# A long convolution beside an MLP: its middle transforms rebuilt from 32x32 tiles

## The chip, the cores and the metric

The kernel runs on one core of one Trainium2 chip. The metric is the device time of one execution in microseconds (us); the median of several runs is given. Beside the runs there is one profiled execution with its own time. PE is the matrix engine TensorE, DVE is VectorE, ACT is ScalarE, POOL is GpSimd, SP is the engine that here only starts DMAs.

## The reference

The input has S = 2048 rows of D = 448 channels, fp32. The output is the input plus two branches, both fed by its layernorm:

```
xn  = layernorm(q)                                   # over the 448 channels
kv  = shift_conv(k, shift_k, 4 taps) * v
y   = causal_conv(kv, ssm_k, 2048 taps, per channel) # by FFT of length 4096
y   = y + kv * ssm_D
out = q + xn * y + mish(xn @ w1 + b1) @ w2           # F = 1792
```

## The kernel before

**The MLP** sets the frame. It goes over 8 chunks of 256 rows and, in each, 7 pairs of 2 x 128 hidden features: 56 pairs of two slots each. A pair's even slot is `g1_mm` (first layer, 22 products 128x256), its odd slot is `mish` on ACT, with the split of the result into a high and a low part (`ach` by ACT, `acl` by DVE), and `g2_mm` of an earlier pair (second layer, 12 products 128x448 into PSUM `pg`). All is fp32 split into two reduced parts, so each layer takes three products.

**The convolution** is put between the MLP's slots by hand. `at(slot, ...)` puts a step before the MLP's part of a slot, `after(slot, ...)` behind it; each engine then runs its instructions in the order in which they are written. It goes in three steps, both for the filter H (`ssm_k`, with `ssm_D` added to its first row) and for V (the product kv):

1. `f1_mm`, `f1_fold`, `f1_out`: the first transform, 8 groups each for H (slots 6 to 32) and V (slots 24 to 59). Its results go through `st` to the DRAM arrays `Dh` and `Dkv`. `taps_pool` (L201) makes one tap of the shift convolution on POOL.
2. Eight *octets* (o = 0 to 7), every third slot from 66 to 87, each with 16 of the 128 rows (of 32 x 448) of Dh and Dkv: `o_load` fetches its `ah` (from Dh) and `av` (from Dkv) on SP's queue; `octet` runs on PE the first inverse step of the octet before (`i1_mm`), then the second transform of H and of V (`f2_mm`); ACT and DVE copy the transformed H to `hs` and the inverse's output to `qe` (`empty`), and `qe` goes to DRAM `E` on POOL's queue; `prod` then multiplies the transformed V, which stays in PSUM, by `hs` on DVE: four products and two sums per octet give the real part `ya` and the imaginary part `yc`, which the next octet's inverse step reads. The last octet's inverse step runs alone at slot 89.
3. `e_load`, `fold`, `i2_mm`, `gate`, `gate_out`: the rest of the inverse at slots 100 and 108, the gate, and an adding store to the output.

[...] `pg` (second layer) has two; three pairs of banks (`duo`: 0, 1 = `pq`, 2 = `pr`) serve the convolution and the first layer. In the octets pair 0 is two single tiles, `pa` and `pb`. `GB` tells which bank the first layer's result of a pair goes to. An odd octet (s odd) stands in a slot whose MLP part begins with a `mish`; that one is run ahead of the octet, and its split is `held` until the products are under way.

The transforms run on parts of the 128x128 array side by side: `f2_mm` takes eight tiles of 64 rows x 32 columns at once for the real, then for the imaginary part of H and of V; `i1_mm` eight tiles of 32 x 64, once for each of its two terms.

Of the kernel before, what the change touches and what calls it, by code (L numbers as in the profile page):

```python
# [7 lines left out]
F32 = mybir.dt.float32  # L8
# [7 lines left out]
NJ = 16  # L16
# [12 lines left out]
OCT_AT = (66, 3)  # L29
# [20 lines left out]
def tile_kernel(ctx: ExitStack, tc, q, qT, k, v, sk, hT, sD, head, w1, w2, c_g, c_gi, c_i2, out):  # L50
# [52 lines left out]
    def bk(p, r):  # L103
        return p[r] if isinstance(p, list) else p[:, r]

    def bank(n):
        return bk(duo[n // 2], n % 2)
# [4 lines left out]
    def regroup(one):  # L112
# [3 lines left out]
        duo[0] = [g1p[0].tile([128, 512], F32, name=n) for n in ("pa", "pb")] if one else g1p[0].tile([128, 2, 512], F32, name="pp")  # L116
# [118 lines left out]
    def o_load(d, src, o, name):  # L235
        if d is AH:
            g = t2([128, 4, 2, 32], "g", 2)
            nc.sync.dma_start(g, c_g[:, o])
            GT[o] = [g]
        d[o] = t2([128, 4, D], name, 2 if d is AV else 1)  # L240
        nc.sync.dma_start(d[o], src[16 * o:16 * o + 16].rearrange("(t a) n d -> (a n) t d", t=4))

    def gi_load(o):
        gi = t2([128, 2, 2, 64], "gi", 2)
        nc.sync.dma_start(gi, c_gi[:, o])
        GT[o].append(gi)

    def f2_mm(a, o, c, n):
        p = pc(n)
        g = GT[o][0]  # L250
        for t in range(4):
            for r in range(2):
                rs = slice(64 * r, 64 * r + 64)
                nc.tensor.matmul(bk(p, r)[32 * t:32 * t + 32, :D], g[rs, t, c], a[rs, t], start=True, stop=True,  # L254
                                 tile_position=(64 * r, 32 * t))
        return p

    def empty(d, p, eng):
        if isinstance(p, list):
            nc.scalar.copy(d[:, 0], p[0][:, :D])  # L260
            V.tensor_copy(d[:, 1], p[1][:, :D])
        else:
            eng(d, p[:, :, :D])  # L263
# [12 lines left out]
    def prod(o):  # L276
        vr, vi = (p[:, :, :D] for p in PS.pop(("V", o)))
        hs = HS.pop(o)
        hr, hi = hs[:, 0], hs[:, 1]
        a, c = Y[o] = [t2([128, 2, D], n) for n in ("ya", "yc")]  # L280
        b, e = [t2([128, 2, D], n) for n in ("yb", "yd")]
        if o == NO - 1:
            V.tensor_mul(a, vr, hr)
            V.tensor_mul(b, vi, hi)
            V.tensor_sub(a, a, b)
            V.tensor_mul(c, vr, hi)
            V.tensor_mul(e, vi, hr)
            V.tensor_add(c, c, e)
        else:
            for x, *y in ((a, vr, hr), (c, vr, hi), (b, vi, hi), (e, vi, hr)):  # L290
                V.tensor_mul(x, *y)
        for fn in held:
            fn()
        held.clear()
        dv(2)
        if o < NO - 1:
            V.tensor_sub(a, a, b)
            dv()
            V.tensor_add(c, c, e)
            dv()  # L300

    def i1_mm(o, ib):
        gi = GT[o][1]
        ps = [pc(n) for n in ib]
        for c in range(2):
            for t in range(4):
                ts = slice(32 * t, 32 * t + 32)
                for r in range(2):
                    nc.tensor.matmul(bk(ps[t // 2], t % 2)[64 * r:64 * r + 64, :D], gi[ts, r, c], Y[o][c][ts, r],  # L309
                                     start=c == 0, stop=c == 1, tile_position=(32 * t, 64 * r))  # L310
        PS["I", o] = ps
        Y.pop(o)

    def i1_out(o):
        qe = t2([128, 4, D], "qe", 2) if o < NO - 1 else t2([128, 2, 2, D], "hs").rearrange("p a b d -> p (a b) d")
        for i, p in enumerate(PS.pop(("I", o))):
            empty(qe[:, 2 * i:2 * i + 2], p, V.tensor_copy if o == NO - 1 and i else nc.scalar.copy)
        for r in range(2):
            k = 8 * (o % 4) + 4 * r
            nc.gpsimd.dma_start(E.rearrange("p (k h) d -> p k h d", h=2)[:, k:k + 4, o // 4], qe[64 * r:64 * r + 64])  # L320

# [366 lines left out]
    at(OCT_AT[0], regroup, True)  # L688
    at(92, regroup, False)
    for o in range(NO):  # L690
        s, d = OCT_AT[0] + OCT_AT[1] * o, OCT_AT[1]
        ib, hb, vb = ((0, 1), (2, 0), (1, 2)) if s % 2 == 0 else ((0, 2), (1, 0), (2, 1))
        (at if o else after)(s - d if o else s - 7, o_load, AH, Dh, o, "ah")
        at(s - d - 1 if o else s - 3, o_load, AV, Dkv, o, "av")
        at(s, octet, o, ib, hb, vb)
        at(s, gi_load, o)
        after(s, prod, o)
        if s % 2:
            hv.add(s)
            GB[s // 2 + 1] = 0  # L700
        else:
            GB[s // 2], GB[s // 2 + 1] = 0, 2
    at(s + 2, i1_mm, o, (1, 2))
    after(s + 2, i1_out, o)
    GB[s // 2 + 2] = 1
# [11 lines left out]
    for i, n in enumerate((0, 4, 0, 4, 2, 4, 2, 0, 2, 4)):  # L717
        GB[46 + i] = n

# [83 lines left out]
    for s in range(nslots):  # L803
# [8 lines left out]
        fns = plan2.pop(s, ())  # L812
        for fn, args in fns:
            if fn is i1_out:
                fn(*args)
        for fn, args in fns:
            if fn is not i1_out:
                fn(*args)
# [5 lines left out]
def _constants():  # L824
# [10 lines left out]
    f1 = np.stack([Wo.real, Wo.imag], axis=4).reshape(64, 128)  # L835
    f1 = np.concatenate([f1, f1])

    i2 = np.stack([W.real.T, W.imag.T])[:, :32].reshape(64, 2, 32) / 2048
    i2 = np.concatenate([i2, i2])
    n2 = np.arange(32)[:, None] // 2 + 16 * (np.arange(32)[:, None] % 2)  # L840
    k2 = np.arange(32)[None, :]
    G = np.zeros((2, 2, 32, 8, 4, 2, 32))
    GI = np.zeros((4, 32, 8, 2, 2, 2, 16, 2))
    for kk in range(64):
        o, r, t = kk // 8, kk // 4 % 2, kk % 4
        g = w(n2 * (4 * kk - 1) + 256 * n2 * k2)
        G[r, 0, :, o, t, 0], G[r, 1, :, o, t, 0] = g.real, -g.imag
        G[r, 0, :, o, t, 1], G[r, 1, :, o, t, 1] = g.imag, g.real

        gt = g.T.reshape(32, 16, 2).transpose(0, 2, 1)  # L850
        GI[t, :, o, r, 0, ..., 0], GI[t, :, o, r, 1, ..., 0] = gt.real, gt.imag
        GI[t, :, o, r, 0, ..., 1], GI[t, :, o, r, 1, ..., 1] = -gt.imag, gt.real
    c = lambda a: np.ascontiguousarray(a, dtype=np.float32)
    return dict(c_f1=c(f1[:, :64]), c_id=c(np.eye(128)), c_g=c(G.reshape(128, 8, 4, 2, 32)), c_gi=c(GI.reshape(128, 8, 2, 2, 64)),
# [37 lines left out]
```

## Time and profile before

| | |
|---|---|
| median of 3 runs | 357.48 us (357.44 to 357.56) |
| profiled execution | 357.13 us, its span 355.4 us |
| PE busy | 99% of the span, granted clock 0.999 |
| DVE, ACT, POOL busy | 80%, 45%, 21% |
| octet 0, octets 1 to 7, last inverse: length on PE | 3.17, 4.92 each, 1.80 us |
| PE time of the octets and the last inverse together | 39.4 us |

Busy times are averages over the whole span. PE's timeline shows where a stretch of the convolution begins and where the MLP's next product begins behind it; the length of a stretch in the table is the time between these two. A row of the timeline gives start, duration, engine, line, operation, output and inputs by the program's names, the part of the array that is used (rows*columns), the output's shape, and the number of instructions; in brackets, the idle time before it and who ended it.

### The profile page before, as it was taken

The page shows a single profiled execution, that of the slowest core. Times are in us where ns is not written, and L with a number is a line of the kernel's source. Part 1 is how long each engine was busy: PE and PEld are TensorE (multiplying, and loading weights), DVE is VectorE, ACT ScalarE, POOL GpSimd, SP SyncE. Part 2 cuts the span into 40 slices and gives each one's busy share as a digit, 9 for nine tenths or more (in the row PEclk, how much of TensorE's full clock was granted, in tenths as well). Part 3 has the DMA queues.
Part 4 walks back from the last instruction along what each step waited for, and adds up shares of the span by engine and source line. Part 5 has one row for each costly group of instructions (what it writes and reads, how often), then busy time and mean ns, then how long its engine had stood idle before and what let it go on. Part 6 is the DMA issues. An engine that isn't in the chain of part 4 may idle for free.

```text
span 355.4 us, 7520 instructions
## 1 busy us (share of the span) xinstructions
PE 351.0 (99%) x3098; PEld 290.2 (82%) x3098; DVE 282.8 (80%) x375; ACT 160.4 (45%) x310; POOL 73.7 (21%) x85
## 2 busy tenths in 40 slices
PE   8999999999999999999999999999999999999996
PEld 3988888888888989888987568658757799979795
DVE  5999658998999998997539868868985963788943
ACT  4966552347343643373232732233634333354480
POOL 3047002822220250222000120110310116040030
PEclk9999999999999999999999999999999999999999
DMA  7999977949769347664869489679755466989176
GB/s 262 370 328 321 410 291 175 344 121 245 207 182 315 126 149 177 216 162 110 245 198 352 122 310 314 224 237 378 252 183 210 105 170 258 406 332 277 28 116 144
DMA packets 30835, 83.27 MB, mean 234 GB/s; under 512 B 3153, under 2 KB 15954, under 8 KB 30802
## 3 DMA queue, kind: packets, MB, share of 16 engines
q1 hardware_dynamic: 21986, 47.78, 39.5%
q0 software_dynamic: 4928, 22.95, 20.7%
q10 hardware_dynamic: 3888, 12.08, 13.1%
q8 instruction: 24, 0.39, 0.4%
q14 instruction: 9, 0.07, 0.1%
HBM read 54.34 MB, written 28.45 MB: 233 GB/s over the span
## 4 chain that ended last, share of the span: by engine, by line
PE 99%; DVE 0%; issue 0%
PE pg L555 24%; PE pg L587 13%; PE pg L589 13%; PE pg L588 12%; PE pa L555 6%; PE pq L555 5%; PE pq L165 4%; PE pa L309 3%; PE pr L555 3%; PE pq L254 3%; PE pr L254 3%; PE pp L555 2%; PE pa L254 1%; PE pg L743 1%; PE pp L363 1%; PE pg L507 1%
## 5 line engine op out<-in xcount | busy, mean ns | idle before, releaser
L587 PE MATMUL pg<-w2h,ach 128*128 128x448 f32 x222 | 81.7, 368 | 0.0
L589 PE MATMUL pg<-w2h,acl 128*128 128x448 f32 x222 | 80.7, 364 | 0.0
L588 PE MATMUL pg<-w2l,ach 128*128 128x448 f32 x222 | 80.5, 363 | 0.0
L98 DVE TENSOR_TENSOR acl<-a,ach 128x512 fp32r<-128x512 f32 x56 | 38.9, 695 | 34.3 <-ACT ach L97 34.2
L555 PE MATMUL pg<-XH,w1h 128*128 128x256 f32 x264 | 52.7, 283 | 0.0
L563 ACT ACTIVATE a<-pg,b1t 128x256 f32<-128x256 f32 x66 | 27.8, 471 | 54.3 <-PE pg L555 43.4
L587 PEld LDWEIGHTS pg<-w2h,ach 128*128 128x128 f32 x222 | 41.6, 188 | 9.4 <-issue 5.0
L555 PEld LDWEIGHTS pg<-XH,w1h 128*128 128x128 f32 x264 | 41.5, 188 | 6.8 <-issue 4.2
L589 PEld LDWEIGHTS pg<-w2h,acl 128*128 128x128 f32 x222 | 41.7, 188 | 2.5
L588 PEld LDWEIGHTS pg<-w2l,ach 128*128 128x128 f32 x222 | 41.8, 188 | 2.3
L555 PE MATMUL pg<-XL,w1h 128*128 128x256 f32 x264 | 43.0, 278 | 0.0
L175 DVE TENSOR_TENSOR st<-pq,st 128x896 f32<-128x896 f32 x32 | 34.8, 1089 | 4.7 <-ACT st L171 3.8
L555 PEld LDWEIGHTS pg<-XL,w1h 128*128 128x128 f32 x264 | 36.0, 188 | 0.0
L97 ACT CAST ach<-a 128x512 fp32r<-128x512 f32 x56 | 34.8, 621 | 1.7
L555 PE MATMUL pg<-XH,w1l 128*128 128x256 f32 x198 | 33.6, 279 | 0.0
L201 POOL TENSOR_TENSOR x<-kr,skb 128x896 f32<-128x896 f32 x8 | 17.0, 2128 | 70.5 <-PE pr L165 26.3
L320 POOL DMA_DIRECT2D E<-qe x14 | 8.8, 630 | 94.4 <-ACT qe L263 94.4
L218 DVE TENSOR_TENSOR x<-x 128x896 f32<-128x896 f32 x24 | 26.2, 1092 | 2.0 <-POOL x L201 1.4
L555 PEld LDWEIGHTS pg<-XH,w1l 128*128 128x128 f32 x198 | 27.7, 189 | 0.0
L171 ACT COPY st<-pr 128x896 f32<-128x896 f32 x16 | 14.5, 906 | 13.5 <-PE pr L165 10.7
L563 ACT ACTIVATE a<-pa,b1t 128x256 f32<-128x256 f32 x16 | 6.7, 471 | 30.5 <-PE pa L555 30.5
L165 PE MATMUL pr<-x,con 32*64 32x448 f32 x128 | 15.9, 560 | 0.0
(191 smaller groups left out, 649.2 us busy)
## 6 DMA issues: line engine op xcount, KB each, us to landing
Dkv<-st ACTq DMA_DIRECT2D x16, 448.0 KB, 5.2
ah<-Dh SPq DMA_DIRECT2D x8, 896.0 KB, 7.6
av<-Dkv SPq DMA_DIRECT2D x8, 896.0 KB, 9.5
e<-E POOLq DMA_DIRECT2D x8, 896.0 KB, 7.3
E<-qe POOLq DMA_DIRECT2D x14, 448.0 KB, 7.2
kr<-in_k_dram SPq DMA_DIRECT2D x10, 448.0 KB, 5.9
Dh<-st ACTq DMA_DIRECT2D x10, 448.0 KB, 6.8
x<-in_v_dram SPq DMA_DIRECT2D x8, 448.0 KB, 6.2
```

Of the source, the lines that this page charges most:

```text
L97: nc.scalar.copy(h, raw)
L98: V.tensor_sub(l, raw, h)
L165: nc.tensor.matmul(ps[h][64 * jj:64 * jj + 64, b, :D], f1[rg:rg + 32], x[rg:rg + 32, jj], start=True, stop=True, tile_position=(rg, 64 * jj))
L175: f(st[:, n], e, st[:, 1])
L201: nc.gpsimd.tensor_mul(o, KR[g - u // 2], skb[:, u:u + 1].to_broadcast([128, 2, D]))
L218: V.tensor_add(KV[g], KV[g], o)
L254: nc.tensor.matmul(bk(p, r)[32 * t:32 * t + 32, :D], g[rs, t, c], a[rs, t], start=True, stop=True, tile_position=(64 * r, 32 * t))
L555: nc.tensor.matmul(ps[n], l, r, start=all(m[0] != n for m in seq[:n_]), stop=all(m[0] != n for m in seq[n_ + 1:]))
L563: nc.scalar.activation(a[:, n], ps[n], AF.Mish, bias=b1t[:, 2 * p + n:2 * p + n + 1])
L587: nc.tensor.matmul(ps, ah[:, n, cs], w2h[:, f], start=f == 0, stop=False)
L588: nc.tensor.matmul(ps, ah[:, n, cs], w2l[:, f], start=False, stop=False)
L589: nc.tensor.matmul(ps, al[:, n, cs], w2h[:, f], start=False, stop=f == NF - 1 or (f == NF - 3 and jj == 1 and c == NCHUNK - 1))
```

## The change

The convolution's middle is computed from two blocks of 1024 rows, each with its own 32 x 32 transform tiles.

- **Layout and `turn`.** Rows are laid out by block (`lay`). The first transform's constants for the second block carry the opposite sign of the imaginary part. Before the octets, `turn` adds one block's transformed filter onto the other's in DRAM: eight DRAM-to-DRAM additions on POOL's queue, two at each of slots 40, 44, 48 and 52, 448 KB each.
- **`o_load`** fetches each of `ah` and `av` in four DMAs of 32 partitions instead of one.
- **`f2_mm`** has 32 x 32 tiles: block b uses rows 64b to 64b + 63 of the array and writes a pair of banks of its own. H's two halves need sixteen tiles; nothing is computed for a separate imaginary pass.
- **`i1_mm`** has 32 x 32 tiles too, and takes four inputs where it took two: the products `sp`, `sr` (first term) and `tp`, `tr` (second term) come in without having been summed over p and r. It has 32 products an octet instead of 16, in halves i = 0 (rows 0 to 63) and i = 1 (rows 64 to 127).
- **`prod`** makes H with real and imaginary parts swapped by two stream shuffles within groups of 32 partitions (`hw` from `hs`), then six products on DVE, one sum on POOL (first term) and one on DVE (second term).
- **Order and copies.** An octet's order on PE is now: H (both blocks), inverse half 0, inverse half 1 first term, V block 0, inverse half 1 second term, V block 1. All four PSUM copies of an octet are 128x896 on ACT (before, ACT and DVE had three each, of 448 and 896). Pair 0 is one tile `pp`; the pairs swap roles between even and odd octets. `qe` has one buffer instead of two.
- The last inverse stays at slot 89, in the function `last`. The special order of octet 7's products is dropped.

The core of the diff:

```diff
 def o_load(d, src, o, name):
...
-        nc.sync.dma_start(d[o], src[16 * o:16 * o + 16].rearrange("(t a) n d -> (a n) t d", t=4))
+        rows = src[16 * o:16 * o + 16].rearrange("(t r c) (n b) d -> b r c n t d", r=2, c=2, b=2)
+        for b in range(2):
+            for r in range(2):
+                rg = 32 * (2 * b + r)
+                nc.sync.dma_start(d[o][rg:rg + 32], rows[b, r])
+
+    def turn(n):
+        rows = Dh[32 * n:32 * n + 32].rearrange("(k c) (n b) d -> b c k n d", c=2, b=2)
+        for c in range(2):
+            nc.gpsimd.dma_start(rows[1, 1 - c], rows[0, c], accum_op=ALU.add)
...
-    def f2_mm(a, o, c, n):
-        p = pc(n)
+    def f2_mm(a, o, b, p):
         g = GT[o][0]
         for t in range(4):
             for r in range(2):
-                rs = slice(64 * r, 64 * r + 64)
-                nc.tensor.matmul(bk(p, r)[32 * t:32 * t + 32, :D], g[rs, t, c], a[rs, t], start=True, stop=True,
-                                 tile_position=(64 * r, 32 * t))
-        return p
+                rg = 32 * (2 * b + r)
+                nc.tensor.matmul(p[32 * t:32 * t + 32, r, :D], g[rg:rg + 32, t], a[o][rg:rg + 32, t], start=True, stop=True,
+                                 tile_position=(rg, 32 * t))
...
-    def octet(o, ib, hb, vb):
-        if o:
-            i1_mm(o - 1, ib)
-            i1_out(o - 1)
-        hs = HS[o] = t2([128, 2, 2, D], "hs")
-        ps = [f2_mm(AH[o], o, c, hb[c]) for c in range(2)]
-        for c in range(2):
-            empty(hs[:, c], ps[c], V.tensor_copy)
-        PS["V", o] = [f2_mm(AV[o], o, c, vb[c]) for c in range(2)]
-        AH.pop(o), AV.pop(o)
...
+    def i1_mm(o, i, p, terms):
         gi = GT[o][1]
-        ps = [pc(n) for n in ib]
-        for c in range(2):
-            for t in range(4):
+        for n in terms:
+            for t in (2 * i, 2 * i + 1):
                 ts = slice(32 * t, 32 * t + 32)
                 for r in range(2):
-                    nc.tensor.matmul(bk(ps[t // 2], t % 2)[64 * r:64 * r + 64, :D], gi[ts, r, c], Y[o][c][ts, r],
-                                     start=c == 0, stop=c == 1, tile_position=(32 * t, 64 * r))
...
+                    for y in range(2):
+                        cg = 64 * r + 32 * y
+                        nc.tensor.matmul(p[cg:cg + 32, t % 2, :D], gi[ts, r, n], Y[o][n][y][ts, r],
+                                         start=n == 0, stop=n == 1, tile_position=(32 * t, cg))
...
+    def octet(o):
+        na, nb = (0, 2) if o % 2 else (2, 0)
+        HS[o] = hs, hw = [t2([128, 2, 2, D], n) for n in ("hs", "hw")]
+        ps = [pc(1), pc(na)]
+        for b in range(2):
+            f2_mm(AH, o, b, ps[b])
+        if o:
+            pi = [pc(nb), pc(na)]
+            i1_mm(o - 1, 0, pi[0], (0, 1))
+        for b in (1, 0):
+            nc.scalar.copy(hs[:, b], ps[b][:, :, :D])
+        if o:
+            i1_mm(o - 1, 1, pi[1], (0,))
+        PS["V", o] = pv = [pc(1), pc(nb)]
+        f2_mm(AV, o, 0, pv[0])
+        if o:
+            i1_mm(o - 1, 1, pi[1], (1,))
+            i1_out(o - 1, 0, pi[0])
+        f2_mm(AV, o, 1, pv[1])
+        if o:
+            i1_out(o - 1, 1, pi[1])
+            e_store(o - 1)
+            Y.pop(o - 1)
+        for b in (1, 0):
+            V.stream_shuffle(hw[:, b], hs[:, b], SWAP)
+        AH.pop(o), AV.pop(o)
 
+    def prod(o):
+        v = [p[:, :, :D] for p in PS.pop(("V", o))]
+        Y[o] = [[t2([128, 2, D], n + m) for m in "pr"] for n in "st"]
+        for n, h in enumerate(HS.pop(o)):
+            p, r = Y[o][n]
+            V.tensor_mul(p, v[0], h[:, 0])
+            V.tensor_mul(h[:, 1], v[0], h[:, 1])
+            V.tensor_mul(r, v[1], h[:, 0])
+            if n == 0:
+                for fn in held:
+                    fn()
+                held.clear()
+                dv()
+            (V if n else nc.gpsimd).tensor_add(r, r, h[:, 1])
+            dv()
...
+        nxt = OCT_AT[o + 1] if o + 1 < NO else I1_LAST
+        for n, i in enumerate(range((s + 1) // 2, (nxt + 1) // 2)):
+            GB[i] = (0 if o % 2 else 4) + n % 2
+
+    def last():
+        p = [pc(1), pc(2)]
+        for i in range(2):
+            i1_mm(NO - 1, i, p[i], (0, 1))
+        for i in range(2):
+            i1_out(NO - 1, i, p[i], V.tensor_copy if i else nc.scalar.copy)
+        e_store(NO - 1)
+
+    at(I1_LAST, last)
```

The instructions' order on PE in octet 2, before (`pa`, `pb`, `pq`, `pr` are PSUM tiles, `gi` and `g` constants; x counts neighbours that read alike):

```order
L309 MATMUL pa<-ya,gi 64x448 x2
L309 MATMUL pb<-ya,gi 64x448 x2
L309 MATMUL pq<-ya,gi 64x448 x4
...
L254 MATMUL pr<-ah,g 32x448 x8
L254 MATMUL pa<-ah,g 32x448
...
L254 MATMUL pq<-av,g 32x448 x8
L254 MATMUL pr<-av,g 32x448 x8
L555 MATMUL pa<-XH,w1h 128x256 x3
```

and now, where `pp` takes the place of `pa` and `pb`, and each row of the inverse that is left out reads like those shown:

```order
L262 MATMUL pq<-ah,g 32x448 x8
L262 MATMUL pr<-ah,g 32x448 x8
L273 MATMUL pp<-sp,gi 32x448
L273 MATMUL pp<-sr,gi 32x448
...
L273 MATMUL pp<-tp,gi 32x448
...
L273 MATMUL pr<-sp,gi 32x448
...
L262 MATMUL pq<-av,g 32x448 x8
L273 MATMUL pr<-tp,gi 32x448
...
L262 MATMUL pp<-av,g 32x448 x8
L563 MATMUL pr<-XH,w1h 128x256 x3
```

The transform of H moved ahead of the inverse, the inverse's second half is split around the first half of V, and the MLP's product behind this octet writes `pr`, which the inverse's second half wrote.

On ACT, octets 2 and 3 before (`hs` transformed H, `qe` inverse output, `a` and `ach` the MLP's activation and its high part):

```order
L260 COPY qe<-pa 128x448
L263 COPY qe<-pq 128x896
L260 COPY hs<-pa 128x448
L563 ACTIVATE a<-pa,b1t 128x256 x2
L97 CAST ach<-a 128x512
L563 ACTIVATE a<-pq,b1t 128x256 x2
L260 COPY qe<-pa 128x448
L263 COPY qe<-pr 128x896
L260 COPY hs<-pa 128x448
L97 CAST ach<-a 128x512
```

and now:

```order
L298 COPY hs<-pr 128x896
L298 COPY hs<-pq 128x896
L279 COPY qe<-pp 128x896
L279 COPY qe<-pr 128x896
L571 ACTIVATE a<-pr,b1t 128x256 x2
L100 CAST ach<-a 128x512
L571 ACTIVATE a<-pr,b1t 128x256 x2
L298 COPY hs<-pp 128x896
L298 COPY hs<-pq 128x896
L279 COPY qe<-pr 128x896
L279 COPY qe<-pp 128x896
L100 CAST ach<-a 128x512
```

ACT has four large copies in a row where it had one large and two small ones, and H comes ahead of the inverse's output.

On DVE, the products of octet 7, whose last sum the last inverse waits for, before:

```order
L261 COPY qe<-pb 128x448
L263 COPY hs<-pq 128x896
L261 COPY hs<-pb 128x448
L283 TENSOR_TENSOR ya<-pr,hs 128x896
L284 TENSOR_TENSOR yb<-pq,hs 128x896
L285 TENSOR_TENSOR ya<-ya,yb 128x896
L286 TENSOR_TENSOR yc<-pr,hs 128x896
L287 TENSOR_TENSOR yd<-pq,hs 128x896
L288 TENSOR_TENSOR yc<-yc,yd 128x896
L98 TENSOR_TENSOR acl<-a,ach 128x512
```

and now:

```order
L312 STREAM_SHUFFLE hw<-hs 128x896 x2
L320 TENSOR_TENSOR sp<-pq,hs 128x896
L321 TENSOR_TENSOR hs<-pq,hs 128x896
L322 TENSOR_TENSOR sr<-pr,hs 128x896
L101 TENSOR_TENSOR acl<-a,ach 128x512
L320 TENSOR_TENSOR tp<-pq,hw 128x896
L321 TENSOR_TENSOR hw<-pq,hw 128x896
L322 TENSOR_TENSOR tr<-pr,hw 128x896
L328 TENSOR_TENSOR tr<-tr,hw 128x896
```

The copies are gone from DVE, two shuffles and two products are added, and the MLP's split `acl` stands between the two terms.

More of the change, by code (lines that the diff above doesn't have):

```diff
@@ L115, in regroup @@
         g1p[0] = psg[0].enter_context(tc.tile_pool(name="ps_g1", bufs=1, space=PSUM, reuse_waits="tile"))
[L116 removed]
+        duo[0] = g1p[0].tile([128, 2, 512], F32, name="pp")
     drip = []
@@ L686, in tile_kernel @@
             after(2 * (p + G2_LAG) - 1, w2_split, p)
[L688 to L695, printed above, removed]
+    for n, t in enumerate(TURN_AT):
+        at(t, turn, n)
+    at(OCT_AT[0], regroup)
+    for o, s in enumerate(OCT_AT):
+        (at if o else after)(OCT_AT[o - 1] if o else s - 7, o_load, AH, Dh, o, "ah")
+        at(OCT_AT[o - 1] - 1 if o else s - 3, o_load, AV, Dkv, o, "av")
+        at(s, octet, o)
         at(s, gi_load, o)
@@ L811, in tile_kernel @@
         mlp_slot(s)
[L812 to L818, printed above, removed]
+        for fn, args in plan2.pop(s, ()):
+            fn(*args)
     assert not plan and not plan2
```

109 lines of the change are left out of this document (38 added, 71 removed).

## The prediction

> **What bounds the kernel now.** I read the page first: the span, PE's share, the granted clock and the chain of waits.
>
> ```profile
> span 355.4 us, 7520 instructions
> PE 351.0 (99%) x3098; PEld 290.2 (82%) x3098; DVE 282.8 (80%) x375; ACT 160.4 (45%) x310; POOL 73.7 (21%) x85
> PEclk9999999999999999999999999999999999999999
> PE 99%; DVE 0%; issue 0%
> ```
>
> TensorE works 99% of the span and is 99% of the chain that ended last, at full clock. So a change is worth what it does to the length of the stretches of PE that it touches, plus any new hole. The changed stretches are the eight octets and the last inverse. The table of windows gives each from its first matmul to the next MLP matmul (octet 0, octets 2, 3 and 7, the last inverse, then the sum of all nine):
>
> ```profile
> 185.68:188.85 3.17, 3.17 (x65) 1.00 (x65) 2.08 (x3) 0.53 (x1) 0.00 (x0) 1.00 0.96 351
> 208.89:213.81 4.92, 4.92 (x98) 1.63 (x97) 2.76 (x4) 1.87 (x3) 1.26 (x2) 1.00 0.63 187
> 221.42:226.34 4.92, 4.92 (x97) 1.56 (x96) 2.69 (x4) 3.23 (x6) 1.24 (x2) 1.00 0.46 142
> 271.74:276.66 4.92, 4.92 (x97) 1.56 (x97) 2.69 (x4) 3.23 (x6) 1.24 (x2) 1.00 0.10 23
> 281.86:283.66 1.80, 1.76 (x34) 0.56 (x33) 1.80 (x4) 1.46 (x3) 0.00 (x0) 1.00 0.00 0
> sum 39.41, PE 39.37 PEld 12.61 DVE 25.32 ACT 21.66 POOL 8.76; mean PE 4.37 PEld 1.40 DVE 2.81 ACT 2.41 POOL 0.97
> ```
>
> PE is busy through each: nothing is waited for there now. The timeline of PE in octet 2 prices a pass (eight tiles side by side; an fp32 product takes two passes):
>
> ```profile
> 208.89 0.59 PE L309 MATMUL pa<-ya,gi 32*64 32x448 f32 x2
> 209.32 0.54 PE L309 MATMUL pa<-ya,gi 32*64 32x448 f32 x2
> 209.69 0.54 PE L309 MATMUL pa<-yc,gi 32*64 32x448 f32 x2
> ...
> 212.11 1.02 PE L254 MATMUL pq<-av,g 64*32 64x448 f32 x16
> 212.86 1.02 PE L254 MATMUL pr<-av,g 64*32 64x448 f32 x16
> 213.81 0.38 PE L555 MATMUL pa<-XH,w1h 128*128 128x256 f32 x1
> ```
>
> The first pass after the MLP takes 0.43, then one each 0.375 (212.86 − 212.11 = 0.75 for two). The last starts at 213.24 and the MLP 0.57 later. A pass's results are complete about 0.55 after its start (the second column). An octet is 12 such passes (octet 0: 8).
>
> **The new octet.** Times below are from its first matmul. I call A the transform of H (L262, sixteen tiles, two passes), B the inverse's first half (four passes on rows 0 to 63), C and E the two terms of its second half (rows 64 to 127), D and F the halves of the transform of V, in the order A B C D E F. Bare passes fill each half of the array eight times, about 3.2 us: a gain of 1.7 an octet if nothing waited. But C goes into the bank that ACT must first empty of H, D into the other one, and F into the bank of B after its copy; PE issues in order, so what stands behind each waits too, the MLP included. All four copies are now 128x896 on ACT. The timeline of ACT in octet 3 prices them:
>
> ```profile
> 221.53 0.84 ACT L563 ACTIVATE a<-pq,b1t 128x256 f32<-128x256 f32 x2 [3.41 <-PE pq L555]
> 223.19 0.53 ACT L260 COPY qe<-pa 128x448 f32<-128x448 f32 x1 [0.82 <-PE pr L309]
> 223.62 0.91 ACT L263 COPY qe<-pr 128x896 f32<-128x896 f32 x1
> ```
>
> One takes 0.91, and the next starts 0.10 before it ends (223.19 + 0.53 against 223.62), so one each 0.81. About 0.06 passes between a matmul's end and the copy it releases, and I allow 0.05 back.
>
> Even octets (2, 4, 6). A: 0, 0.43; complete 1.04 with sixteen tiles. Copies of H: 1.10 to 2.01 and 1.91 to 2.82. B runs under them, 0.8 to 2.5. C starts at 2.06, D at 2.87. E stands behind D: about 2.95 and 3.33, complete 3.88. Copy of B 2.72 to 3.63, F from 3.70. The last copy must wait for E: 3.94 to 4.85. After an even octet the MLP's first product goes into that very bank, so it begins at about 4.95: **+0.03 each, +0.1 together**.
>
> Odd octets (1, 3, 5, 7). The Mish before them ends 0.95 into the octet (221.53 + 0.84 − 221.42) and frees B's bank: B 1.05, 1.45, 1.83, 2.20, complete 2.75; its copy 2.81 to 3.72; F 3.78 and 4.16; the MLP, here a second-layer product into another bank, at 4.16 + 0.57 = 4.73: **−0.19 each, −0.76 together**.
>
> Octet 0 has no inverse. D waits for the second copy, 2.87; F runs beside it on the other rows; second pass 3.25, MLP 3.82 to 3.84 instead of 3.17: **+0.67**.
>
> [...]
>
> **The last inverse.** It stays two slots behind octet 7, which are 5.20 us of MLP (281.86 − 276.66). So PE reaches it at 4.73 + 5.20 = 9.93. Its second term now needs two shuffles, six products and a sum, all but one sum on DVE. DVE's timeline:
>
> ```profile
> 213.27 1.09 DVE L291 TENSOR_TENSOR ya<-pq,hs 128x896 f32<-128x896 f32 x1
> 214.28 1.08 DVE L291 TENSOR_TENSOR yc<-pq,hs 128x896 f32<-128x896 f32 x1
> ...
> 204.84 0.68 DVE L98 TENSOR_TENSOR acl<-a,ach 128x512 fp32r<-128x512 f32 x1
> 205.44 1.08 DVE L297 TENSOR_TENSOR ya<-ya,yb 128x896 f32<-128x896 f32 x1
> ...
> 281.38 1.09 DVE L288 TENSOR_TENSOR yc<-yc,yd 128x896 f32<-128x896 f32 x1
> 282.38 0.69 DVE L98 TENSOR_TENSOR acl<-a,ach 128x512 fp32r<-128x512 f32 x1
> ```
>
> An operation each 1.0 (214.28 − 213.27), the split 0.6 (205.44 − 204.84), and about 1.1 where one needs the one just before. A shuffle is not in this trace: no less than the 0.69 of a 128x512 operation, no more than POOL's 2.14 for 128x896 (quoted below); I take 1.0, the other 128x896 rows of its engine. Then: shuffles 2.06, 3.06; products 4.06, 5.06, 6.06; split 7.06; products 7.67, 8.67, 9.67; sum 10.78 to 11.87. Before, that sum ended at 282.47, ahead of the term that read it:
>
> ```profile
> 276.66 0.47 PE L587 MATMUL pg<-w2h,ach 128*128 128x448 f32 x1
> ...
> 281.86 0.61 PE L309 MATMUL pq<-ya,gi 32*64 32x448 f32 x4
> 282.67 0.56 PE L309 MATMUL pq<-yc,gi 32*64 32x448 f32 x4
> 283.66 0.48 PE L587 MATMUL pg<-w2h,ach 128*128 128x448 f32 x1
> ```
>
> Now the first half's second term waits at 11.92, and the whole second half of the inverse is queued behind it: passes 12.0, 12.4, 12.75, 13.13, MLP at 13.70. Length 3.77 instead of 1.80: **+1.97**. With the shuffle's ends it is +1.3 to +4.2.
>
> [...]
>
> **What I cost at nothing.** The product loop: octet start to sixth product 10.2 (even) or 10.8 (odd), and the next octet starts 12.3 later, so 1.5 of cover. POOL's sum, the eight DRAM additions, the split loads and the single buffer of the inverse's output rest on these rows:
>
> ```profile
> 160.24 2.14 POOL L201 TENSOR_TENSOR x<-kr,skb 128x896 f32<-128x896 f32 x1
> 162.42 1.09 DVE L218 TENSOR_TENSOR x<-x 128x896 f32<-128x896 f32 x1 [0.87 <-POOL x L201]
> 338.65 0.84 POOL L388 DMA_DIRECT2D out_dram<-q  x1 [16.61 <-ACT q L383]
> DMA  7999977949769347664869489679755466989176
> ah<-Dh SPq DMA_DIRECT2D x8, 896.0 KB, 7.6
> E<-qe POOLq DMA_DIRECT2D x14, 448.0 KB, 7.2
> ```
>
> POOL's sum takes 2.14 and is done 9.3 into the octet, read after 12. The additions are issued at slots 40 to 52, about 121 to 155 us by where the MLP stands then, at 0.84 each as the adding stores are, on a POOL that is 79% idle; queued behind them is L201, which DVE waits for. At worst the two of one slot delay a KV group by 1.7, less the 0.5 by which its last step led its transform: +1.2. DMA is at 30 to 70% there. A split load of H must still land in the 12 us between octets; the rows say 7.6, and that of octet 1 comes when DMA is busiest, up to +1. A store of an octet's output, issued about 4.9 into it and landing 7.2 after its issue, is out by 13.4; the buffer is written again at 12.3 + 2.8 = 15.1.
>
> **Sum**: +0.1 − 0.76 + 0.67 + 1.97 = +1.98. From the profiled execution, 357.13 (span 355.4 and 1.7 around it), 359.1; the median of the runs is 0.35 above that execution, 357.48, so the forecast is **359.4**. Its own range, by the shuffle's lower end (−0.65), by 0.15 an octet either way (1.05) and by a longer shuffle (+0.4): 358.2 to 360.9.
>
> **Rivals.** A measurement of this kernel tells about 0.2%, 0.7 us, from no change: 356.8 to 358.2.
>
> 1. Sixteen small tiles don't run together: if only eight go at once, the 16 tile groups of an octet cost 16 passes, 0.43 + 15 × 0.375 + 0.19 = 6.2, +1.3 × 7; octet 0 then costs +2.1 and the last inverse about +1.8: 370.5. For it: no row shows more than eight tiles. Against: tiles of one pass start some 7 ns apart, so issue has room. Chance 0.06.
> 2. The moved traffic is late (KV behind the additions, octet 1's load): +1 to +2.2 on top, 360.4 to 361.6. Against: the cover above. 0.12.
> 3. The copies don't hold PE: if the banks come free early enough, octets take 3.24 and give 7 × 1.68 = 11.8 back, less octet 0's and the last inverse's (which then waits 1.5 longer): about 349.8. The 0.91 rows speak against, unless copies overlap more than by 0.10. 0.07.
> 4. The ends of the sum fall kindly: a shuffle near 0.69 saves 0.65 and octets 0.2 to 0.3 shorter (the last copy's wait for E missing) save 1.5 to 2: about 357.2, no change that can be told. 0.25.
>
> The forecast has 0.50, of which 0.02 falls within 0.2%; case 4 has 0.25, of which 0.18 falls within and 0.07 below. So slower by over 0.2%: 0.48 + 0.06 + 0.12 = 0.66; within: 0.20; faster: 0.07 + 0.07 = 0.14. The range, 356.8 to 361.4, takes in most of 2 and 4 and leaves out 1, 3 and their neighbours.
>
> **What would show it.** Right: in PE's timeline an idle of about 0.8 before C and between C and D, released by ACT's H copies; octets of 4.9 (even) and 4.7 (odd); octet 0 at 3.8; a hole of 2 us inside the last inverse, released by DVE's sum; ACT's four copies back to back but for the last. Wrong: passes of 0.75 in A (rival 1), PE idle on the load of H or on KV (2), no hole at C (3). If DVE is not idle before a shuffle, its loop and not ACT sets the octets, and the sum's first two terms fall.

## The result, and the profile after

The changed kernel takes 372.75 us (median of 4 runs, 371.75 to 373.72) against 357.52 for the kernel before: a ratio of 1.0425, 95% interval 1.039 to 1.0459. I had forecast 359.4 and a range up to 361.4. The sign was right, the size was not: +15.2 us instead of +1.9. The executions of the kernels with the new octets scatter by 2 us and more, in part with PE's mean clock: without the additions (below), 364.44 us at a clock of 0.999 and 369.55 at 0.986.

The page of the changed kernel (its profiled execution took 371.75 us):

```profile
span 370.0 us, 8130 instructions
PE 355.1 (96%) x3354; PEld 294.2 (80%) x3354; DVE 291.7 (79%) x392; ACT 171.8 (46%) x318; POOL 99.5 (27%) x101
PEclk9999999999999999989998999999999999999999
DMA  7999977759687799895999998899977456979276
PE 72%; DVE 10%; issue 6%; DMA 6%; ACT 3%; POOL 2%; SPq 0%; ACTq 0%
```

PE no longer fills the span: it is 72% of the chain of waits. DVE, DMA and ACT now stand in it too, the clock dips twice (slices 18 and 22 of the 40), and the DMA engines are at 80% or more in slices 15 to 29, but for slice 19, where before they were at 40 to 90%.

The table of windows, the same stretches as before (octets 0 to 7, then the last inverse):

```profile
191.67:196.14 4.47, 2.47 (x66) 0.48 (x65) 2.26 (x4) 1.71 (x2) 0.00 (x0) 0.89 1.07 236
204.88:209.85 4.97, 4.83 (x129) 1.60 (x129) 3.85 (x7) 4.50 (x7) 0.00 (x0) 1.00 0.90 188
217.37:224.69 7.32, 5.13 (x129) 2.04 (x128) 4.58 (x7) 3.43 (x4) 0.00 (x0) 1.00 1.03 192
232.41:237.37 4.96, 4.96 (x129) 1.80 (x128) 2.75 (x5) 4.04 (x6) 0.00 (x0) 1.00 0.75 176
244.89:250.12 5.23, 5.03 (x129) 2.22 (x128) 3.35 (x6) 3.43 (x4) 0.00 (x0) 1.00 0.81 207
270.78:276.36 5.58, 5.38 (x129) 2.23 (x129) 5.34 (x9) 3.94 (x5) 0.00 (x0) 1.00 0.54 99
294.11:298.15 4.04, 3.60 (x66) 1.08 (x65) 3.97 (x6) 0.71 (x1) 0.00 (x0) 1.00 0.22 52
```

Octet 0 starts at 191.67 where it started at 185.68: **6.0 us are lost before the octets begin.** From there to the end of octet 1 the kernel before needs 201.37 − 185.68 = 15.69, the changed one 18.18: +2.5. Octet 2 costs +2.4, octets 3 to 7 together +1.4, the last inverse +2.2. That is 14.5 of the 14.6 by which the spans differ. (Octets 5 and 6, 5.26 and 5.58, are the longest of these five: ACT has a cast of 0.62 for the MLP's next chunk there, ahead of the Mish in octet 5 and of the copies of H in octet 6, so that the first copy starts 1.62 into octet 6 where it starts 1.26 into octet 4.)

**The 6.0 us.** PE's timeline at group 6 of the KV transform:

```profile
160.65 0.69 PE L165 MATMUL pq<-x,con 32*64 32x448 f32 x2 [4.37 <-DVE x L221]
```

DVE's timeline, from which the operand comes:

```profile
138.17 0.68 DVE L101 TENSOR_TENSOR acl<-a,ach 128x512 fp32r<-128x512 f32 x1
146.11 1.42 DVE L502 TENSOR_TENSOR xn<-xn,con 128x512 f32<-128x512 f32 x2 [7.26 <-DMA con<-MR]
```

POOL's timeline, SP's timeline, and the groups of DMAs between 120 and 160 us (KB each, us to landing):

```profile
126.58 0.81 POOL L493 DMA_DIRECT2D MR<-mv  x1 [0.31 <-POOL mv L489]
```
```profile
138.24 0.33 SPq L496 DMA_DIRECT2D con<-MR  x1
```
```profile
Dh<-Dh POOLq DMA_DIRECT2D x8, 448.0 KB, 13.9
MR<-mv POOLq DMA_DIRECT2D x1, 2.0 KB, 11.6
```

The MLP's layernorm sends the mean and scale of a chunk through DRAM (`MR`) to have them as a row. That 2 KB store is issued at 126.58, between the first additions, and lands 11.6 later. In the kernel before, its reader on SP's queue was issued at 132.08 instead of 138.24. DVE, which runs in order, stands 7.26 us for the row; the KV products behind it come late, and PE waits 4.37. Then the clock is at half:

```profile
160.65:161.40 0.75, 0.75 (x16) 0.23 (x16) 0.75 (x2) 0.72 (x3) 0.00 (x0) 0.75 1.03 165
161.40:162.10 0.70, 0.70 (x11) 0.01 (x1) 0.70 (x2) 0.66 (x3) 0.00 (x0) 0.50 1.05 297
164.50:165.00 0.50, 0.50 (x4) 0.48 (x3) 0.50 (x2) 0.50 (x1) 0.25 (x1) 1.00 0.89 322
```

The column before the last two is the granted clock: 0.50 from 161.0 to 164.4. That costs the transform and the MLP behind it the other 1.6 us.

**Octet 2.** ACT, which copies out octet 1's inverse there, waits for the store of octet 0's from the same buffer, and PE waits for ACT:

```profile
222.82 0.91 ACT L279 COPY qe<-pp 128x896 f32<-128x896 f32 x1 [2.47 <-DMA E<-qe]
```

The second half of that store was issued at 211.06 and landed 11.66 later, where 7.2 was the median before, and 8.4 the time of this very half.

### The profile page after: what moved, and what is told of

It reads as the page before. It is cut to its first block, busy times and chain, and to the rows that moved or that the text cites. A ratio compares the mean times of both kernels' runs of the same rounds, so it can differ in the third digit from the quotient of the medians.

```text
span 370.0 us, 8130 instructions
## 1 busy us (share of the span) xinstructions
PE 355.1 (96%) x3354; PEld 294.2 (80%) x3354; DVE 291.7 (79%) x392; ACT 171.8 (46%) x318; POOL 99.5 (27%) x101
## 4 chain that ended last, share of the span: by engine, by line
PE 72%; DVE 10%; issue 6%; DMA 6%; ACT 3%; POOL 2%; SPq 0%; ACTq 0%
PE pg L563 18%; PE pg L595 10%; PE pg L597 10%; PE pg L596 10%; PE pr L563 6%; PE pp L563 4%; PE pq L165 4%; DMA E<-qe 3%; PE pq L563 2%; PE pr L273 2%; PE pq L262 2%; DVE hw L312 2%; DMA MR<-mv 2%; DMA x<-in_head_dram 1%; PE pp L273 1%
## 5 line engine op out<-in xcount | busy, mean ns | idle before, releaser
L328 POOL TENSOR_TENSOR sr<-sr,hs 128x896 f32<-128x896 f32 x8 | 18.3, 2288 | 36.8 <-DVE sr L322 36.8
L571 ACT ACTIVATE a<-pr,b1t 128x256 f32<-128x256 f32 x24 | 10.0, 469 | 28.8 <-PE pr L563 28.8
L165 PE MATMUL pq<-x,con 32*64 32x448 f32 x128 | 16.4, 576 | 4.7 <-DVE x L221 4.4
```

The lines of the kernel that those rows point to most:

```text
L165: nc.tensor.matmul(ps[h][64 * jj:64 * jj + 64, b, :D], f1[rg:rg + 32], x[rg:rg + 32, jj], start=True, stop=True, tile_position=(rg, 64 * jj))
L328: (V if n else nc.gpsimd).tensor_add(r, r, h[:, 1])
L571: nc.scalar.activation(a[:, n], ps[n], AF.Mish, bias=b1t[:, 2 * p + n:2 * p + n + 1])
```

## The experiments

Medians of four runs are given, and behind them the ratio to the kernel before, measured at the same time, with its 95% interval; where there is one run only, the stretches of its profile decide.

### Is it the additions, and by which way?

Without them:

```diff
-            nc.gpsimd.dma_start(rows[1, 1 - c], rows[0, c], accum_op=ALU.add)
+            pass
```

> The changed kernel without its eight DRAM additions: one block's transformed filter is not added to the other's, so the output lacks that part; all else stays. Theory (the statistics row queues behind the additions in POOL's DMA queue, DVE waits for it, the KV product and group 6 of its transform come 4.4 us late and PE's clock drops behind the hole): the hole of 4.4 and the slow stretch of 1.6 behind it are gone, 372.75 to about 366.7. Rival (the hole comes from something else that the change moved): still about 372.7.

367.42 us (1.0283, 1.0227 to 1.034), 5.3 less. The KV transform has no hole, and octet 0 starts at 185.70 instead of 191.67: the 6.0 us are gone.

The additions alone, put into the kernel before, onto an array of their own:

```diff
+        rows = Dh[32 * n:32 * n + 32].rearrange("(k c) (n b) d -> b c k n d", c=2, b=2)
+        ru = Du[32 * n:32 * n + 32].rearrange("(k c) (n b) d -> b c k n d", c=2, b=2)
+        for c in range(2):
+            nc.gpsimd.dma_start(ru[1, 1 - c], rows[0, c], accum_op=ALU.add)
```

> The kernel before, with the same eight additions at the same four slots but into a DRAM array that nothing reads. Theory (the additions alone do it): a hole of some 4.4 us ahead of group 6 of the KV transform and a slow clock behind it, 357.5 to about 363.5. Rival (it takes the changed octets' loads or layout as well): within 1 us of 357.5.

363.98 us (1.0195, 1.0166 to 1.0223), 6.8 more. DVE's timeline has the same wait, and PE's the hole:

```profile
146.03 1.42 DVE L502 TENSOR_TENSOR xn<-xn,con 128x512 f32<-128x512 f32 x2 [6.63 <-DMA con<-MR]
```
```profile
160.57 0.59 PE L167 MATMUL pq<-x,con 32*64 32x448 f32 x2 [3.76 <-DVE x L223]
```

Octet 0 starts at 191.46, and octets 1 to 7 take 4.92 as before. So the additions do it with no help from the rest of the change. My theory was that the small store queues behind them in POOL's queue:

```diff
-        nc.gpsimd.dma_start(MR[c].rearrange("j (p t) -> p j t", t=2), mv[:, 2 * c:2 * c + 2])
+        nc.sync.dma_start(MR[c].rearrange("j (p t) -> p j t", t=2), mv[:, 2 * c:2 * c + 2])
```

> The changed kernel with all additions, but the layernorm statistics rows of chunks 3 to 7 are stored by SP's DMA queue instead of POOL's. Theory (order in POOL's queue): as without the additions, about 366.7, with DVE's wait of 7.26 us for the row gone. Rival (the additions only fill the DMA engines, whoever issues the store): the row is late all the same and the time stays within 1.5 us of 372.75.

379.91 us (376.59 to 387.57; 1.0639, 1.057 to 1.0708), worse. The group of the store between 120 and 160 us reads

```profile
MR<-mv SPq DMA_DIRECT2D x1, 2.0 KB, 11.6
```

11.6 as before, where the other four of these stores on SP's queue land after 3.6 to 5.5: **that theory fell.** Moving the store to another queue did not free it. The additions fill the DMA engines themselves: in the changed kernel the packets of all queues add up to 1.04 to 1.34 of the engines' time in each 5 us from 123 to 148, against 0.23 to 0.91 in the kernel before, and the small store among them is late. In what way the additions hold up a store that is on another queue, no run shows. (SP now also stands waiting for the statistics, 60.7 us for the five stores, and the loads behind them in its queue wait too. That this is the rest of the loss was not tested.)

If it is a collision, other slots should help. Slots 43, 45, 47 and 49 leave the store of chunk 4 ahead of the additions and that of chunk 5 behind them:

```diff
-TURN_AT = (40, 44, 48, 52)
+TURN_AT = (43, 45, 47, 49)
```

> The changed kernel with its additions at slots 43, 45, 47 and 49 instead of 40, 44, 48 and 52, so that chunk 4's statistics are stored ahead of all of them and chunk 5's behind them. Theory (whatever round trip falls among the additions is late; it was the statistics of chunk 4): DVE's wait of 7.26 for that row is gone or under 2, the hole ahead of KV group 6 shrinks to under 2, 368 to 370. Rival (the DMA engines are full in any case and the loads of k and v are as late as the row): the hole stays at 3 or more, 371 to 374.

366.0 us (1.026, 1.0229 to 1.0292), 6.7 less with all additions still there, and better than I expected: the hole ahead of group 6 is gone, and 0.3 is left ahead of group 7. It was their place, not their work.

### The octet loads

```diff
-        rows = src[16 * o:16 * o + 16].rearrange("(t r c) (n b) d -> b r c n t d", r=2, c=2, b=2)
-        for b in range(2):
-            for r in range(2):
-                rg = 32 * (2 * b + r)
-                nc.sync.dma_start(d[o][rg:rg + 32], rows[b, r])
+        rows = src[16 * o:16 * o + 16].rearrange("(t a) (n b) d -> b a n t d", t=4, b=2)
+        for b in range(2):
+            nc.sync.dma_start(d[o][64 * b:64 * b + 64], rows[b])
```

> The changed kernel with each octet load in two DMAs of 64 partitions instead of four of 32. Theory A (the 1792-byte packets of the octet loads take 127 ns instead of 74 because of the small DMAs): they come back towards 74 to 90 ns, the store of the first inverse lands sooner, octet 2 loses its hole of 2.2: about 370.5. Rival B (every other row of 1792 bytes, or the load on the DMA engines as a whole, makes the packets slow): 110 ns or more, octet 2 keeps its hole, 372 to 373.

373.95 us (1.0465, 1.0409 to 1.0521): no gain. The 1792-byte packets of SP's queue still have a median of 136 ns (126 in the changed kernel, 74 before; medians over the packets of that size between 180 and 300 us of each trace). Four DMAs or two makes no difference to them. The hole was not where the rival had it: octet 2 takes 5.24, and octet 3 takes 8.03, where ACT waits 2.42 for the store of the inverse's output. So the same loads, every other row, went into the kernel before:

> The kernel before, whose octet loads fetch every other row of 1792 bytes in two DMAs of 64 partitions, as the changed kernel has to (the rows then meet the wrong constants: this leaves the transform without its right order, the work is the same). Theory (the access to every other row makes the packets slow): the 1792-byte packets of the octets take 125 to 140 ns instead of 74, and with them the early octets' loads and stores are later; the time is 357.5 to 359.5, since the kernel before has two buffers for the inverse's output. Rival (the packets are slow because of the changed kernel's other traffic): 74 to 90 ns and no change.

360.61 us (1.0107, 1.0063 to 1.0151): +3.3, more than expected, with packets of 128 ns. PE's octets wait for H there (us in total, times, longest; the last line is the landing of `ah`, 7.6 in the median before):

```profile
PEld pr L256 <- DMA ah<-Dh: 2.4, 3, 1.2
PEld pq L256 <- DMA ah<-Dh: 2.2, 4, 0.7
DMA to landing us min/median/max: 8.0/9.9/11.3
```

So loads of every other row, in two DMAs, have packets that take some 70% longer (128 ns against 74), with nothing else changed. I put that down to the new order of rows; two DMAs of adjacent rows were not run, so the cut of one load into several is not excluded by itself.

### The octets themselves

Both reasons for slow DMAs taken out, additions and row order (one load in the old order, nothing else changed):

> The changed kernel without the additions and with each octet load as one DMA in the row order of the kernel before (the rows then meet the wrong constants and one block's filter part is missing; the work on the engines is the same). Theory (additions and every-other-row loads are the DMA part of the loss, and the engines' own part is octet 0, the octets and the last inverse): no hole in the KV transform, the 1792-byte packets back to 74 to 90 ns, octets 1 and 2 at 4.96 and 5.24 like the undisturbed ones, octet 0 at 4.0 and the last inverse at 4.0; 357.4 + 0.85 + 4 x 0.04 + 3 x 0.32 + 2.2 = 361.6 us. Rival (the holes in octets 1 and 2 come from the order on the engines): they stay, 364 or more.

365.03 us (1.0208, 1.0181 to 1.0235). The table of windows of this kernel:

```profile
185.40:189.86 4.46, 2.45 (x66) 0.48 (x65) 2.23 (x5) 1.71 (x2) 0.00 (x0) 0.90 1.00 361
198.62:203.60 4.98, 4.80 (x130) 1.53 (x129) 3.82 (x7) 4.48 (x7) 0.00 (x0) 1.00 0.51 158
211.13:216.37 5.24, 5.17 (x130) 1.97 (x129) 3.37 (x6) 3.53 (x4) 0.00 (x0) 1.00 0.70 163
236.46:241.69 5.23, 5.03 (x129) 2.14 (x128) 3.36 (x6) 3.43 (x4) 0.00 (x0) 1.00 0.55 184
285.76:289.80 4.04, 3.60 (x65) 1.08 (x65) 3.97 (x6) 0.72 (x1) 0.00 (x0) 1.00 0.21 50
```

The packets are back at 74 ns and octet 2 has no hole (5.24); odd octets take 4.96 to 5.27, even ones 5.23 to 5.83: the stretches that I had expected but for octets 5 and 6 (5.27 and 5.83). The time is above the 361.6 expected: the profiled execution took 363.38, the three others 364.9 to 365.6, and for these no trace exists. In the profiled one, 18.20 us pass from the start of octet 0 to the end of octet 1; 1.6 of them are the wait of octet 1 that is taken apart below. The drop of the clock behind octet 0 (0.90 in the first line) is not what it pays for: without the additions there is no drop, and the same two octets take 18.06. **No octet is shorter than before, with the DMAs out of the way.** Why? PE's timeline of octet 3 in the changed kernel (start 232.41; the inverse's rows between 233.4 and 235.4 and beside D are left out), then ACT's:

```profile
232.41 0.60 PE L262 MATMUL pq<-ah,g 32*32 32x448 f32 x8
232.54 0.61 PE L262 MATMUL pp<-ah,g 32*32 32x448 f32 x8
232.81 0.58 PE L262 MATMUL pq<-ah,g 32*32 32x448 f32 x8
...
235.44 0.61 PE L262 MATMUL pq<-av,g 32*32 32x448 f32 x8
236.28 1.16 PE L262 MATMUL pr<-av,g 32*32 32x448 f32 x16
237.37 0.47 PE L595 MATMUL pg<-w2h,ach 128*128 128x448 f32 x1
```
```profile
233.67 0.91 ACT L298 COPY hs<-pp 128x896 f32<-128x896 f32 x1 [0.32 <-issue]
234.48 0.91 ACT L298 COPY hs<-pq 128x896 f32<-128x896 f32 x1
235.27 0.93 ACT L279 COPY qe<-pr 128x896 f32<-128x896 f32 x1
236.69 0.91 ACT L279 COPY qe<-pp 128x896 f32<-128x896 f32 x1 [0.49 <-PE pp L273]
```

Sixteen tiles do run at once: the passes of A are 0.40 apart. But rows 64 to 127 are empty from about 0.9 to 2.22, until the first copy of H is done; then six passes stand there (C, E, F), 2.22 to 4.96. Two runs ask whether that copy or ACT's whole chain sets the end. The second copy of H on DVE:

```diff
-            nc.scalar.copy(hs[:, b], ps[b][:, :, :D])
+            (nc.scalar.copy if b else V.tensor_copy)(hs[:, b], ps[b][:, :, :D])
```

> The changed kernel with the second copy of H on DVE, beside the first on ACT. Theory A: D starts at 2.4 instead of 3.03, but the six passes behind the first copy stay, so an undisturbed octet is 4.85 to 4.96 as before. Theory B (ACT's chain): one copy fewer in it, octets shorter by 0.6 to 0.8, 4.2 to 4.4.

D starts at 2.52 instead of 3.03, and octets 3 and 7 take 4.93 instead of 4.96. (One run, 369.4 us.) ACT's chain is not it. Octet 0, which has no inverse, does get shorter, 3.32 instead of 4.02; octet 1 then waits until 14.44 after the start of octet 0, as it did without this. And the first copy cut in halves:

```diff
+            if b:
+                nc.scalar.copy(hs[:, b, 0], ps[b][:, 0, :D])
+                V.tensor_copy(hs[:, b, 1], ps[b][:, 1, :D])
+            else:
+                nc.scalar.copy(hs[:, b], ps[b][:, :, :D])
```

> The changed kernel with the first of the two copies of H cut in halves, one on ACT and one on DVE at the same time. Theory A (rows 64 to 127 stand idle until the first copy of H, and six passes follow it): C starts at 1.9 instead of 2.22, undisturbed octets are shorter by 0.25 to 0.3 (4.96 to 4.7). Theory B (the chain of ACT's four copies, as forecast): ACT's chain is shorter by 0.4, octets by 0.4. Rival C (PE's passes alone): no change.

It missed (one run, 372.69 us). DVE's half did not run beside ACT's (DVE's timeline of octet 7, and the window of that octet):

```profile
286.24 0.62 DVE L300 COPY hs<-pp 128x448 f32<-128x448 f32 x1 [2.45 <-ACT hs L299]
```
```profile
284.41:289.60 5.19, 5.19 (x129) 2.25 (x128) 3.32 (x6) 3.73 (x6) 0.00 (x0) 1.00 0.11 40
```

DVE waited for ACT, so the first copy ended 0.28 later, C began at 2.51, and octets 3 and 7 take 5.19: +0.23. Half a microsecond earlier at the second copy gives 0.03, 0.29 later at the first costs 0.23: the first copy and the six passes behind it leave no room.

In the odd octets that path is not alone. The weight loads of octet 3 in the changed kernel, for C and for F:

```profile
234.63 0.10 PEld L273 LDWEIGHTS pp<-sp,gi 32*32 32x32 f32 x1 [0.27 <-ACT hs L298]
236.25 0.39 PEld L262 LDWEIGHTS pr<-av,g 32*32 32x32 f32 x16 [0.42 <-ACT qe L279]
```

F was released by the copy of B (236.20, the end of the third row of ACT above), as forecast, and E's second pass had begun 0.38 before F, a pass apart. The two paths end together. With the second copy of H on DVE, F still waits for B's copy, and that copy for PE (0.64), not for ACT's other copies: B itself stands behind the Mish. To shorten an odd octet both paths would have to be shorter; no run here did that.

### Octet 1

In nine of the eleven profiles with the new octets B of octet 1 starts 14.3 to 14.5 us after octet 0 does. (14.8 where the first copy of H was split; the last is the test below.) First, octet 0 with V's second block ahead of its first, on top of the later additions:

> The changed kernel with the additions at slots 43 to 49 and, in octet 0 alone, V's second block ahead of its first: the second block's bank is free from the start, so PE has 0.75 us of passes to do while ACT copies H. Theory (the drop of PE's clock behind octet 0 needs a hole of about 2 us): the hole is 1.2, octet 0 stays at 4.0 because its first block still waits for the second copy, and the clock stays at 1.0 behind it; about 365.5 against 366.0. Rival (the drop comes whatever the hole): the clock is 0.5 for 3.4 us behind octet 0 all the same, 366 or more.

365.7 us (1.0223, 1.0189 to 1.0256) against 366.0: no difference that can be told. The hole in octet 0 shrank to 1.0, octet 0 stayed at 3.96 and no drop followed it, as the theory had it; but behind the hole of 2.0 in the run it is compared with none followed either, so that part is not shown. In both the drop came in octet 1 (here the clock is 0.80 over its 7.97 us), and B begins 14.4 after octet 0 in both. Its chain stands in the timelines of DVE, ACT and PE and in octet 1's window (from 197.45), here with the later additions and the old order in octet 0:

```profile
196.31 1.09 DVE L328 TENSOR_TENSOR tr<-tr,hw 128x896 f32<-128x896 f32 x1
197.32 1.49 DVE L502 TENSOR_TENSOR xn<-xn,con 128x512 f32<-128x512 f32 x2
```
```profile
198.84 0.62 ACT L509 CAST XH<-xn 128x512 fp32r<-128x512 f32 x1 [4.70 <-DVE xn L502]
199.37 0.83 ACT L571 ACTIVATE a<-pr,b1t 128x256 f32<-128x256 f32 x2
```
```profile
200.25 0.56 PE L273 MATMUL pr<-sp,gi 32*32 32x448 f32 x1 [1.69 <-ACT a L571]
```
```profile
197.45:205.49 8.04, 6.35 (x130) 2.90 (x129) 6.40 (x10) 4.84 (x8) 0.00 (x0) 0.79 1.09 211
```

DVE does octet 0's products, then the normalise step of chunk 5; ACT's cast waits for that, the Mish stands behind the cast, and B of octet 1 needs the bank that Mish reads. The test takes that step out of the chain:

```diff
-NT_HOW[5] = dict(NT_AT, q=-8, stats=-4, flush=-2)
+NT_HOW[5] = dict(NT_AT, q=-8, stats=-4, flush=-2, row=(3, 6), norm=(5, 9), split=(6, 10))
```

> The changed kernel with the additions at slots 43 to 49 (366.0), and chunk 5's normalisation two to four slots earlier, so that its second half stands ahead of octet 0's products on DVE instead of behind them, and its cast ahead of octet 1's Mish by three slots on ACT. Theory (octet 1 waits for a chain: octet 0's products on DVE, the normalise step behind them, the cast on ACT, the Mish behind it, which frees the bank of B; in seven profiles B of octet 1 begins 14.3 to 14.5 after the start of octet 0): B of octet 1 begins 1.0 to 1.3 after octet 1's start, its stretch is 5.0 instead of 8.0, no clock drop in it, 363 to 364. Rival (octet 1 waits for its loads, which are made of every other row): B's wait and the 8.0 stay, about 366.

363.89 us (363.01, 363.14, 364.64 and 368.89; 1.0184, 1.0153 to 1.0216), as expected, and B begins 12.63 after octet 0, 1.00 into octet 1:

```profile
185.84:189.86 4.02, 2.01 (x65) 0.48 (x64) 3.01 (x6) 2.23 (x3) 0.00 (x0) 1.00 1.11 219
197.48:202.44 4.96, 4.96 (x129) 1.79 (x128) 3.90 (x7) 4.05 (x6) 0.00 (x0) 1.00 1.11 209
209.96:216.46 6.50, 5.14 (x130) 2.04 (x129) 4.58 (x7) 3.43 (x4) 0.00 (x0) 1.00 1.05 261
```

Octet 1 is 4.96 and the clock stays at 1.00; the wait for the inverse's store is back in octet 2 (6.50, its store landing after 10.8). This is the best version found with the whole computation, still 1.8% slower than the kernel before. Neither a second buffer for that store nor this together with the second copy of H on DVE was run.

### The last inverse

```diff
-I1_LAST = 89
+I1_LAST = 90
```

> The changed kernel with the last inverse one slot later (90 instead of 89). Theory (PE waits 2 us inside it for DVE's last sum): the hole goes and its stretch is 1.9 to 2.0 instead of 4.04, the time 372.75 to about 370.7; the runs of the changed kernel scatter over 2 us, so the stretch decides. Rival (its 32 products cost more passes than counted): the stretch stays above 3.

372.44 us (1.0449, 1.0409 to 1.049): no gain, and the theory missed. The stretch is 3.38, full of work, at a clock of 0.79. About 0.7 of it is the clock (an estimate: 1.44 us at half of it); the other 2.7 is still more than 1.9 to 2.0, since most of the second half's products begin 1.7 behind the first half's and not beside them. And PE has waited earlier:

```profile
293.27 0.47 PE L595 MATMUL pg<-w2h,ach 128*128 128x448 f32 x1 [2.66 <-DVE qt L602]
```

A second-layer product needs a bank that DVE must empty (`qt`), and that step stands on DVE behind octet 7's products. The loss is DVE's queue; PE can wait for it in one place or in the other.

## Why the prediction was wrong

- **"What I cost at nothing", the additions: the step that failed most.** I priced their issue on POOL (0.84 each; 0.9 to 1.0 measured) and the DMA engines by their busy share of 30 to 70%. I did not ask who else waits for a small transfer there. The 2 KB store of the statistics landed after 11.6 instead of 4.9, DVE stood 7.26 for its row and PE 4.37 for DVE. The additions cost 5.3 to 6.8 us by three runs. Rival 2 named the additions, but by POOL's queue and at +1.2.
- **The split loads**: priced by count and median landing. The order of the rows was not priced; it costs 3.3 us alone in the kernel before, and by my reading makes stores late with it (octet 2).
- **The store's single buffer**: I took the median landing, 7.2, and 1.7 of cover; it landed after 11.7, and ACT waited 2.47.
- **The product loop, "1.5 of cover"**: the chain by DVE's products alone was right (about 10), but the normalise step, the cast and the Mish stand behind them on the same engines. From octet 0 to the end of octet 1 it cost +2.5 instead of +0.5.
- **Octets**: even 4.95 forecast, 5.23 measured; odd 4.73, 4.96. The mechanism for the even ones (the last copy waits for E, the MLP for the copy) held. Sixteen tiles complete at 1.11, not 1.04, and the first copy starts 0.15 behind that, not 0.06: C at 2.22 instead of 2.06. For the odd ones the term named held too: the copy of B ends at 3.79 (3.72 forecast) and releases F at 3.87 (3.78), and from F to the MLP it is 1.09 instead of 0.95. What the forecast did not see is that the first copy of H and the six passes behind it end at the same time.
- **Octet 0 and the last inverse held**: +0.85 at full clock against +0.67, and +2.24 against +1.97; the shuffles are 1.1 apart instead of 1.0. The +0.4 for a longer shuffle, at the upper end of the forecast's own range, is a term that no run shows: two shuffles at 1.1 make +0.2.
- **Rival 1** (tiles not at once) is out: passes of 0.40. **Rival 3** is out: even without the DMAs' part no octet gained.
- **The bare passes' gain**, 1.7 an octet and 12 us over seven, never came. The second copy of H on DVE beside the first on ACT gave 0.03 in octets 3 and 7, where two paths end together, and 0.70 in octet 0, which has no inverse.
- **Missing altogether**: the clock behind a hole, 1.6 us at group 6.
- The lower end of the forecast's own range is not added up as the upper one is: 359.4 − 0.65 − 1.05 is 357.7, not 358.2. Nothing rests on it.

What stays open: the other executions of the kernel with the engines alone are 1.5 to 2.2 longer than the profiled one; the store's wait in octet 2 was not isolated by a run of its own (its second half lands after 9.6 us and octet 2 takes 5.24 with both reasons for slow DMAs out, 10.0 and 5.63 without the additions alone); whether the order of the rows or their cut into several DMAs makes the packets slow.

## What to carry to other kernels

Price a bulk DMA by who else has a transfer in the air while it runs, above all small round trips through DRAM that an in-order engine waits for (here 2 KB that landed after 11.6 us instead of 4.9, and DVE stood 7.26 for the row); a mean busy share does not show that, the landing times of the small ones do, and another slot can be worth more than another queue (366.0 us against 379.91). Halving the passes of a stretch gave nothing here (octets of 4.96 and 5.23 us against 4.92) while PSUM copies stood in front of most of what was left; where two chains end together, shortening one shows nothing. When an engine's chain is lengthened, write down all that stands behind it on that engine and on the next, not only the loop itself.

## What the runs showed of the hardware

PE's clock falls to 0.50 behind some holes. In the changed kernel it does so for 3.41 us at a time, from 161.02 and from 195.15. A pass takes nearly twice as long in that time (0.74 instead of 0.40 in the last inverse at slot 90). It costs only where PE would not wait anyway: 1.6 us behind group 6, but next to nothing behind octet 0 (18.18 us from its start to the end of octet 1 with the drop, 18.06 without the additions, where there is none). Holes of 4.37 (group 6), 2.66 (ahead of the last inverse at slot 90), 2.0 (octet 0 of the changed kernel, and with the engines alone) and 1.72 (octet 1, with octet 0 in its other order) were followed by a drop; holes of 2.0 (octet 0 without the additions, with the later ones, and with the earlier normalise step) and one of 2.19 (octet 2 of the changed kernel) were not. So their length alone does not decide it. In the changed kernel's trace drops begin at 161.02, 195.15 and, in the last microsecond of the span, 369.23. PE was idle for 3.04, 2.00 and 2.58 us of the 3.41 just ahead of these three. The hole of 2.19 lies between the last two, where the clock stays at 1.00. What decides it, no run shows.

In the changed kernel a DRAM-to-DRAM addition of 448 KB lands in 13.9 us among its like, and its 1792-byte packets have a median of 159 ns, against 74 for plain ones of that size and 126 to 136 where every other row is fetched.

Two copies of H, on ACT and DVE, from two PSUM tiles into two halves of `hs` ran side by side (282.27 to 283.18 and 282.14 to 283.23 in octet 7, with the second copy on DVE). Two from the two banks of one PSUM tile into two quarters of it ran one after the other: DVE waited for the end of ACT's copy (285.68 to 286.21, DVE's from 286.24 in octet 7), an order that the program sets; no run shows whether the engines could have done both at once.
